# Decay matrix of one attention chunk from a broadcast load instead of matmuls, with a new order table, in a fused mLSTM and two-MoE kernel

## The chip, the cores and the metric

The kernel runs on one core of a Trainium2 chip. A core has TensorE (PE in the profile; PEld is its weight load), VectorE (DVE), ScalarE (ACT), GpSimd (POOL) and SyncE (SP), which here only issues DMAs. The metric is the device time of one execution in microseconds, lower is better.

## The reference, cut to what matters

Three layers follow each other. The first is an attention with gates, written in the reference as a recurrence over 768 tokens for 2 batches and 8 heads of width 40:

```python
for t in range(S):
    m_new = np.maximum(f_gate[:, :, t] + m, i_gate[:, :, t])
    f_stab = np.exp(f_gate[:, :, t] + m - m_new)
    i_stab = np.exp(i_gate[:, :, t] - m_new)
    C = f_stab * C + i_stab * outer(v_t, k_t)
    n = f_stab * n + i_stab * k_t
    y[:, :, t] = sigmoid(o_gate_t) * (C @ q_t) / max(abs(n . q_t), 1)
```

Its 1536 rows of 320 go through `rms` normalisation and a SwiGLU layer (`w_gate`, `w_val` 320x1536, `w_out` 1536x320), and then through a PReLU layer (`w_in` 320x2048, `w_out` 2048x320). The result is 1536x320 in float32.

## The kernel before, in words

The attention is done in 6 chunks of 128 tokens, each for 2 batches: twelve units `u`. For a unit and a head the recurrence becomes a 128x128 matrix of weights `w` (the decay from one token to another, the exponential of a difference of running sums, masked to the past), which multiplies the scores (`sc`, L448) and then the values (`pv`, L502); a state `st` of 40x41 per head carries what lies before the chunk (`pv` from the state at L471, its update at L526). A unit is then normalised on DVE, ACT and POOL, turned on PE (`trxn`, L624) and split into a high and a low half (`xh`, `xl`), since all matmuls of the two MoE layers are made of three products of fp32r halves.

The first MoE layer multiplies per chunk and per pair `p` of 256 columns (`moe1_pair`, L781: 16 products into `g`, 16 into `v`), takes tanh, multiplies, splits the result (`gh` on ACT at L793, `gl` on DVE or POOL at L796) and multiplies by the out weights (`moe1_out`, L787). Chunks 0 and 1 go through it together, since their weights are being made at that time: each block of weights is loaded raw (L662), and ACT and DVE (in part POOL) make its two halves from it (`decode`, L666 to L694). The second MoE layer has 3 x 16 blocks of 512 columns in the same manner (`moe2_chunk`, `moe2_out`).

The decay matrices are made in two ways. With `NB = 2`, chunks 0 and 1 build theirs on PE (`spread` in `prep`, L379 to L391): a product of an identity with a triangular mask (L381), four products that spread a row of `sp` over 128 rows (L384) and one that spreads a column (L389). `sp` holds the running sums of 16 heads as high half in rows 0 to 15 and low half in rows 32 to 47 of 48; ACT writes the high halves (L283), DVE the low ones (L281). One ACT exponential of 128x512 finishes half a unit (L396). From chunk 2 on, the running sums `gA` are written to DRAM (`a_scr`, L318), loaded back to 128 partitions with a broadcast (`load_A`, L407, 512 KB), masked on POOL (L355) and exponentiated per head on ACT with the column as bias (L363); `cols` (L286) then turns one more 16x16 block on PE, and `out_e` copies the column out.

Everything is written as steps of a plan: each call `plan(engine, cost, fn, w, r, take)` gives a step a number, what it writes and reads, and which buffer it takes. Buffers that matter here: 2 of `w`, 2 of `vko` (one load of 484.5 KB per unit), 4 of `r` (two loads of 160 KB per unit), 3 of `stg` (raw weights, mostly 512 KB per load), 1 of `gate`. The order in which the steps are issued is not worked out by the kernel but stands in a table, `ORDER` (from L1024): a number is a step, a trailing `g` puts a step that may run on DVE or POOL on POOL, and `*n` issues `n` filler matmuls of 128 columns (`idle`, L1015, tile `hot`), which are two PE instructions each. Each engine takes its own steps in the order of the table and waits by semaphores for what it reads.

Of the kernel before, what the change touches and what calls it, by code (L numbers as in the profile page):

```python
# [116 lines left out]
def kernel(  # L117
# [15 lines left out]
    nc = tc.nc  # L133
# [58 lines left out]
    def consts():  # L192
# [30 lines left out]
        plan("V", 300, sel, w="sel sp0 sp1", r="ident")  # L223
# [8 lines left out]
    def gates_of(c):  # L232
# [53 lines left out]
        def cols():  # L286
            ps = new(f"gc{c}", "ps", [128, 512])
            if c >= NB:
                nc.tensor.transpose(ps[:, 0:G], T[gt][:, 0, :], ident[:G, :G])
            if c:  # L290
                nc.tensor.transpose(ps[:, G:2 * G], T[gA], ident[:G, :G])
            if 0 < c < NB:
                nc.tensor.matmul(ps[0:DT, 2 * G:3 * G], lhsT=sp_t[c][:, 0, C - 1:C].to_broadcast([48, DT]), rhs=sel_t,
                                 start=True, stop=True)
# [39 lines left out]
    def prep(u):  # L334
# [39 lines left out]
        if c < NB:  # L374
            dec_of(lambda rows, h: T[f"gc{c}"][rows, 2 * G + b * H + h:2 * G + b * H + h + HP, None], f"gc{c}" if c else "")
            for s in range(2):
                ab = f"ab{u}_{s}"

                def spread(ab=ab, s=s):  # L379
                    ps = new(ab, "ps", [128, 4, C])  # L380
                    nc.tensor.matmul(ps, lhsT=idr, rhs=tri_t[:, None, :].to_broadcast([128, 4, C]), start=True, stop=False)  # L381
                    for i in range(4):
                        g = b * H + 4 * s + i
                        nc.tensor.matmul(  # L384
                            ps[:, i], lhsT=sel_t[:, g:g + 1].to_broadcast([48, 128]), rhs=sp_t[c][:, 0],
                            start=False, stop=False
                        )
# [12 lines left out]
                plan("P", tuple(sum(x) for x in zip(mm(1, 512), mm(4, 128, rows=48), mm(1, 512, rows=48))), spread,  # L400
# [3 lines left out]
        else:  # L404
# [31 lines left out]

    def scores(u):
# [15 lines left out]
        plan("P", half(mm(H, 128, rows=40, pairs=True)), prod, w=f"sc{u}_0 sc{u}_1", r=f"{r}/0 {r}/1",  # L453
# [4 lines left out]
    def before(u):  # L458
# [24 lines left out]
        plan("P", half(mm(H, 41, rows=40, pairs=True)), prod, w=f"pv{u}_0/b pv{u}_1/b", r=f"{r}/0 {r}/1 st{b}",  # L483
             take=[("ps", f"pv{u}_{s}", KEEP) for s in range(2)])
        for s in range(2):
# [539 lines left out]
3 7 18 0 19 20 1 2 162 170 26 27 8 9 28 13 5 10 178 11 77 12 14 4 15 16 90 17 *9 35 91 76 99 100 40 21 354 355 163 23  # L1025
22 164 166 171 165 31 172 190 174 24 167 173 168 56 198 25 175 36 169g 176 29 366 37 61 367 34 179 177 38 30 6 32 180
182 33 39 58 55g 57 78 181 *1 53 41 206 44 83g 42 79 59 54 43 80 45 343 81 46 183 60 82 48 184 188 47 *1 74 186 62 191
65 63 84 49 64 86 85 92 109 192 75 87 199 66 185 67 88 200 68 189 187 201 *3 50 93 342 102 89 202 110 214 69 111 133
70 194 207 101 94 203 51 193 204 52 222 119 71 195 95 344 196 205 96 72 208 210 73 348g 215 209 103 97 230 197 146 211
216 105 104 98 217 212 108 112 223 213 106 224 107 135g 132 577 231 114 578 113 117 134 218 238 345 219 115 118 220  # L1030
346 226 566 221 *1 136 232 116 347 123 350 120 349 121 *1 139 160g 137 239 138 122 234 124 225 125 357 159 589 141 126
# [6 lines left out]
456 464 263g 471 465 466 264 458 424 473 472 277 474 298 265g 291 478 475 425 284 279 476 504 285 280 477 286 505 506
310 281 299 292 507 287 490 489 508 288 492 293 509 482 289 300 302 294 311 483 318 301 484 326 295 485 510g 296 491
486 479 480 297 487 481 312 314 493 488 319 567 313 500 495 334 568 494 571 496 303g 327 315 304 502 501 497 308 316  # L1040
522 306 305 498 503 524 320 322 309 523 499 307 428 335 321 525 591 512 430 1117 323 511 514 317 324 513 328 330 515
325 336 338 329 638 516 1125 337 517 518 1133 339g 1118 519 526 520 331 340 521 332 341 527 528 1126 333 1119 529 1127
# [3 lines left out]
685 542 588 703 600 651 686 633 601g 632 627g 636 687 704 705 543 706 555 707 605 556 607 557 606 602 559 560 608 603  # L1046
# [6 lines left out]
791 781 792 812g 813 824 793 782 828 838 794 783 829 795 830 784 840 796 797 839 798 864 803 800 801 802 804 805 841  # L1053
# [100 lines left out]
```

## Time and profile before

| | |
|---|---|
| median of 3 runs | 486.62 us (485.04 to 491.96) |
| the profiled execution | 487.92 us |
| its span, first to last instruction | 486.1 us |
| mean granted TensorE clock | 0.947 |
| PE busy | 479.6 us, 3410 matmuls |
| DVE, ACT, POOL busy | 337.7, 206.8, 58.9 us |

Busy times are the union of an engine's instructions. Matmuls are pipelined, so the own time of one overlaps the next; the distance from one start to the next start is what a matmul costs PE. The granted clock of a stretch is 1.00 (2.4 GHz) or 0.50 (1.2 GHz).

### The profile page before, as it was taken

The page shows a single profiled execution, that of the slowest core. Times are in us where ns is not written, and L with a number is a line of the kernel's source. Part 1 is how long each engine was busy: PE and PEld are TensorE (multiplying, and loading weights), DVE is VectorE, ACT ScalarE, POOL GpSimd, SP SyncE. Part 2 cuts the span into 40 slices and gives each one's busy share as a digit, 9 for nine tenths or more (in the row PEclk, how much of TensorE's full clock was granted, in tenths as well). Part 3 has the DMA queues.
Part 4 walks back from the last instruction along what each step waited for, and adds up shares of the span by engine and source line. Part 5 has one row for each costly group of instructions (what it writes and reads, how often), then busy time and mean ns, then how long its engine had stood idle before and what let it go on. Part 6 is the DMA issues. An engine that isn't in the chain of part 4 may idle for free.

```text
span 486.1 us, 8659 instructions
## 1 busy us (share of the span) xinstructions
PE 479.6 (99%) x3410; PEld 448.2 (92%) x3410; DVE 337.7 (69%) x651; ACT 206.8 (43%) x419; POOL 58.9 (12%) x83
## 2 busy tenths in 40 slices
PE   8999999999999999999999999999999999999997
PEld 7888999999999999999999999889988999898987
DVE  4788788898745745754568799999537475555753
ACT  4485496667471326213525677535103131121211
POOL 1320223231030102102012021202000000000000
PEclk9555699999999999999899999999999999999999
DMA  6864554356520250043006546521001000010001
GB/s 224 300 200 149 200 168 144 105 182 221 142 87 18 70 173 1 19 138 104 34 1 160 178 131 190 166 71 49 1 1 57 15 16 2 0 42 13 1 0 55
DMA packets 18184, 46.56 MB, mean 96 GB/s; under 512 B 2400, under 2 KB 7392, under 8 KB 18144
## 3 DMA queue, kind: packets, MB, share of 16 engines
q1 hardware_dynamic: 18144, 46.01, 29.9%
q8 instruction: 27, 0.44, 0.4%
q14 instruction: 13, 0.11, 0.1%
HBM read 39.02 MB, written 4.36 MB: 89 GB/s over the span
## 4 chain that ended last, share of the span: by engine, by line
PE 93%; DMA 2%; DVE 2%; ACT 1%; issue 0%; POOL 0%; POOLq 0%
PE hm L781 18%; PE accm L787 17%; PE g L781 13%; PE acc L787 13%; PE v L781 12%; PE pv L502 5%; PE sc L448 3%; PE pv L471 2%; PE hot L1018 2%; DMA raw1169w<-in_wi 2%; PE ab L384 2%; PE stp L526 2%; PE trxn L624 1%; PE ab L381 1%; DMA raw1177w<-in_wo 1%; PE ab L389 1%
## 5 line engine op out<-in xcount | busy, mean ns | idle before, releaser
L793 ACT ACTIVATE ghm<-tm 128x512 fp32r<-128x512 f32 x48 | 30.3, 633 | 109.7 <-PE accm L787 90.0
L796 DVE TENSOR_TENSOR glm<-tm,ghm 128x512 fp32r<-128x512 f32 x45 | 30.9, 689 | 41.2 <-ACT ghm L793 35.3
L880 DVE TENSOR_SCALAR tm<-hm,al_sb 128x512 f32<-128x512 f32 x48 | 35.9, 749 | 8.2 <-PE hm L781 6.3
L819 DVE SCALAR_TENSOR_TENSOR t<-t,g 128x512 f32<-128x512 f32 x36 | 24.6, 685 | 21.6 <-ACT t L816 21.2
L816 ACT ACTIVATE t<-g 128x512 f32<-128x512 f32 x36 | 21.4, 595 | 40.1 <-PE g L781 32.8
L793 ACT ACTIVATE gh<-t 128x512 fp32r<-128x512 f32 x36 | 22.4, 630 | 28.0 <-PE acc L787 16.0
L886 DVE SCALAR_TENSOR_TENSOR tm<-hm,tm 128x512 f32<-128x512 f32 x48 | 32.8, 688 | 1.0
L822 DVE SCALAR_TENSOR_TENSOR t<-t,v 128x512 f32<-128x512 f32 x36 | 24.4, 684 | 10.3 <-PE v L781 9.6
L796 DVE TENSOR_TENSOR gl<-t,gh 128x512 fp32r<-128x512 f32 x34 | 24.0, 715 | 9.8 <-ACT gh L793 9.8
L502 PEld LDWEIGHTS pv<-vko,w 128*128 128x128 f32 x192 | 28.4, 229 | 0.8 <-issue 0.4
L502 PE MATMUL pv<-vko,w 128*128 128x41 f32 x192 | 28.8, 313 | 0.0
L363 ACT ACTIVATE w<-w,col 128x128 f32<-128x128 f32 x64 | 20.0, 394 | 0.4 <-DVE col L297 0.3
L452 DVE TENSOR_TENSOR w<-sc,w 128x512 f32<-128x512 f32 x24 | 15.6, 685 | 5.0 <-PE sc L448 3.6
L448 PE MATMUL sc<-r 40*128 40x128 f32 x192 | 17.9, 325 | 0.0
L787 PE MATMUL acc<-o10h,gh 128*128 128x320 f32 x48 | 16.1, 335 | 1.2 <-DVE t L819 1.2
L448 PEld LDWEIGHTS sc<-r 40*128 40x128 f32 x192 | 15.5, 224 | 1.7 <-issue 0.8
L787 PE MATMUL acc<-o12h,gh 128*128 128x320 f32 x48 | 15.9, 331 | 0.0
L787 PE MATMUL acc<-o11h,gh 128*128 128x320 f32 x48 | 15.4, 320 | 0.0
L787 PE MATMUL accm<-o21h,ghm 128*128 128x320 f32 x48 | 15.2, 316 | 0.0
L787 PE MATMUL accm<-o23h,glm 128*128 128x320 f32 x48 | 14.9, 311 | 0.1
L787 PE MATMUL accm<-o20h,glm 128*128 128x320 f32 x48 | 14.9, 311 | 0.0
L787 PE MATMUL accm<-o23h,ghm 128*128 128x320 f32 x48 | 14.9, 310 | 0.0
(498 smaller groups left out, 1647.2 us busy)
## 6 DMA issues: line engine op xcount, KB each, us to landing
vko<-in_vko SPq DMA_DIRECT2D x12, 484.5 KB
w<-a_scr SPq DMA_DIRECT2D x8, 512.0 KB
r<-in_qk SPq DMA_DIRECT2D x24, 160.0 KB
y_scr<-y SPq DMA_DIRECT2D x12, 192.0 KB
x<-y_scr SPq DMA_DIRECT2D x12, 192.0 KB
out<-y SPq DMA_DIRECT2D x12, 160.0 KB
raw206w<-in_wo SPq DMA_DIRECT2D x1, 640.0 KB
raw214w<-in_wo SPq DMA_DIRECT2D x1, 640.0 KB
```

What stands on the lines that cost most here:

```text
L363: nc.scalar.activation(out=T[w][:, h], in_=T[w][:, h], func=AF.Exp, bias=T[f"col{c}"][:, g:g + 1])
L448: nc.tensor.matmul(T[f"sc{u}_{s}"][:, i], lhsT=q[:, 1, i], rhs=q[:, 0, i], start=True, stop=True)
L502: nc.tensor.matmul(ps[:, i, 0:V1], lhsT=T[w][:, h], rhs=v[:, h], start=True, stop=True)
L781: nc.tensor.matmul(ps, lhsT=a, rhs=x, start=(i == 0), stop=(i == len(ops) - 1))
L787: nc.tensor.matmul(a[:, 0:DM], lhsT=g[:, sl], rhs=w[:, j % 4], start=(j == 0 and k == 0), stop=(j == nj - 1 and k == 2))
L793: nc.scalar.activation(out=new(gh, "gh", [128, n], F32R), in_=T[t], func=AF.Copy)
L796: on[e].tensor_tensor(out=new(gl, "gl", [128, n], F32R), in0=T[t], in1=T[gh].bitcast(F32), op=ALU.subtract)
L816: nc.scalar.activation(out=new(t, "t", [128, 512]), in_=T[g], func=AF.Tanh, scale=0.5)
L819: nc.vector.scalar_tensor_tensor(out=T[t], in0=T[t], scalar=1.0, in1=T[g], op0=ALU.add, op1=ALU.mult)
L822: nc.vector.scalar_tensor_tensor(out=T[t], in0=T[t], scalar=0.5, in1=T[v], op0=ALU.mult, op1=ALU.mult)
L880: nc.vector.tensor_scalar(out=new(t, "t", [128, 512]), in0=T[ps], scalar1=0.0, scalar2=al_sb[:, j:j + 1], op0=ALU.min, op1=ALU.mult,)
L886: nc.vector.scalar_tensor_tensor(out=T[t], in0=T[ps], scalar=0.0, in1=T[t], op0=ALU.max, op1=ALU.add)
```

## The change

`NB` becomes 1: chunk 1's decay matrices come by the path of the later chunks (store of `gA`, broadcast load, mask, eight exponentials per unit), and its `spread` steps, its `sp` tile and the `sp` halves go. `sel` and the remaining `sp` tile have 128 rows instead of 48, of which the added ones are zero, so that chunk 0's spreads contract over 128 rows. In `attend` a unit's scores come ahead of its product with the state. The order table is new from end to end.

```diff
-    sel_t = att.tile([48, G], F32R, name="sel")
+    sel_t = att.tile([128, G], F32R, name="sel")
-    NB = 2
-    sp_t = [att.tile([48, 2, C], F32R, name=f"sp{c}") for c in range(NB)]
+    NB = 1
+    sp_t = [att.tile([128, 2, C], F32R, name=f"sp{c}") for c in range(NB)]
...
-                            ps[:, i], lhsT=sel_t[:, g:g + 1].to_broadcast([48, 128]), rhs=sp_t[c][:, 0],
+                            ps[:, i], lhsT=sel_t[:, g:g + 1].to_broadcast([128, 128]), rhs=sp_t[c][:, 0],
                             start=False, stop=False
...
-                        ps, lhsT=sp_t[c][:, 1], rhs=sel_t[:, g:g + 4, None].to_broadcast([48, 4, C]), start=False, stop=True
+                        ps, lhsT=sp_t[c][:, 1], rhs=sel_t[:, g:g + 4, None].to_broadcast([128, 4, C]), start=False, stop=True
...
-                (weighted_v, u), (before, u), (scores, u), (pv, u, 0), (pv, u, 1), (combine, u),
+                (weighted_v, u), (scores, u), (before, u), (pv, u, 0), (pv, u, 1), (combine, u),
...
-3 7 18 0 19 20 1 2 162 170 26 27 8 9 28 13 5 10 178 11 77 12 14 4 15 16 90 17 *9 35 91 76 99 100 40 21 354 355 163 23
+7 0 2 3 1 *4 8 9 10 11 13 14g *7 12 166 174 *1 167 15 168 175 176 77 16 170 17 169 171 177 178 23 21 172 22 24 173 179
...
```

Read by their steps, the two tables give PE this order up to the first product of the first MoE layer (`g0_0`; `u` are units, `I` a filler, a spread is half a unit, a `pv` is half a unit):

```
before: 9 I, sc u0, spread u0, spread u0, spread u1, sc u1, spread u1, pv u0, pv u0, I, state u0,
        pv u1, pv u1, I, state u1, before u2, cols 1, 3 I, turn u0, spread u2, turn u1, spread u2,
        spread u3, spread u3, sc u2, state u2, pv u2, pv u2, I, before u3, I, sc u3, state u3, g0_0
after:  12 I, spread u0, spread u0, sc u0, spread u1, spread u1, sc u1, pv u0, pv u0, pv u1, pv u1,
        state u0, state u1, cols 1, turn u0, sc u2, before u2, turn u1, sc u3, 6 I, g0_0
```

On SP the first loads before are gates, `r` of u0 (two), `vko` of u0, two raw weight blocks; after, gates, two raw weight blocks, `r` of u0 (two). Chunk 1's store and its two broadcast loads stand at places 14, 19 and 28 of SP's queue; the copies that finish the first weight block at 25 and 26, and the gates of chunk 2 ahead of them at 24. On ACT, the decays and four of the eight exponentials of u2 stand ahead of the high half of u1's turned rows. The upper half of chunk 0's `sp` is written on ACT behind the first instruction that reads a raw weight block. Of the 84 low halves `gl` of both MoE layers POOL made 5 before and makes 39 after; of the 39 low halves of weights 3 and 10, of the 39 roundings 6 and 16.

## Rows read from the trace of the kernel before

**Rows 1.** The page: busy time by engine, and PE's granted clock in 40 slices
```profile
PE 479.6 (99%) x3410; PEld 448.2 (92%) x3410; DVE 337.7 (69%) x651; ACT 206.8 (43%) x419; POOL 58.9 (12%) x83
...
PEclk9555699999999999999899999999999999999999
```
**Rows 2.** Waits of PE: engine, line, releaser: us, times, longest
```profile
PE hot L1018 <- POOL ident masks.py:199: 1.7, 1, 1.7
PE acc L787 <- DVE t L819: 1.2, 1, 1.2
```
**Rows 3.** Stretches: length, busy of PE, PEld, DVE, ACT, POOL, PEclk, DMA share, GB/s
```profile
6.70:10.10 3.40, 3.40 (x26) 2.44 (x26) 0.43 (x1) 1.60 (x4) 0.00 (x0) 1.00 0.99 374
10.10:57.90 47.80, 47.80 (x272) 41.03 (x272) 37.72 (x91) 28.50 (x61) 9.92 (x12) 0.50 0.65 209
...
238.80:242.20 3.40, 3.40 (x19) 3.40 (x17) 1.18 (x2) 0.10 (x1) 0.00 (x0) 0.50 0.00 0
```
**Rows 4.** Timeline of PE, 0 to 54: start, own time, operation, count
```profile
1.70 4.21 PE L1018 MATMUL hot<-ident 128*128 128x128 f32 x18 [1.70 <-POOL ident masks.py:199]
5.84 1.86 PE L448 MATMUL sc<-r 40*128 40x128 f32 x16
...
16.72 3.63 PE L502 MATMUL pv<-vko,w 128*128 128x41 f32 x16
20.15 0.78 PE L1018 MATMUL hot<-ident 128*128 128x128 f32 x2
...
27.01 1.93 PE L471 MATMUL pv<-st,r 40*128 40x41 f32 x16
...
29.35 1.65 PE L1018 MATMUL hot<-ident 128*128 128x128 f32 x6
30.79 0.85 PE L624 MATMUL trxn<-ident,xn 128*128 128x128 f32 x3
31.29 0.78 PE L381 MATMUL ab<-tri,idr 128*128 128x512 f32 x1
...
33.57 0.90 PE L624 MATMUL trxn<-ident,xn 128*128 128x128 f32 x3
...
50.44 2.08 PE L448 MATMUL sc<-r 40*128 40x128 f32 x16
...
53.46 0.58 PE L781 MATMUL g<-xh,w10h 128*128 128x256 f32 x1
```
**Rows 5.** Timeline of PE, 70 to 78, at the full clock
```profile
71.70 0.66 PE L526 MATMUL stp<-wv,vko 128*64 128x41 f32 x16
...
72.77 1.09 PE L471 MATMUL pv<-st,r 40*128 40x41 f32 x16
...
76.78 0.98 PE L502 MATMUL pv<-vko,w 128*128 128x41 f32 x8
```
**Rows 6.** Waits of PE's weight loads
```profile
PEld ab L384 <- issue: 3.1, 8, 0.4
```
**Rows 7.** Timelines of SP and ACT, 0 to 14: the first loads and their first reader
```profile
1.53 1.73 SPq L344 DMA_DIRECT2D r<-in_qk  x2
...
3.83 0.42 SPq L662 DMA_DIRECT2D raw162w<-in_wgv  x1
...
8.97 0.67 ACT L666 ACTIVATE raw162w<-raw162w 128x512 f32<-128x512 f32 x1 [0.90 <-DMA raw162w<-in_wgv]
```
**Rows 8.** Waits of POOL, and ACT's exponentials by line (busy, mean ns, idle before)
```profile
POOL w L355 <- DMA w<-a_scr: 4.6, 1, 4.6
...
L363 ACT ACTIVATE w<-w,col 128x128 f32<-128x128 f32 x64 | 20.0, 394 | 0.4 <-DVE col L297 0.3
```
**Rows 9.** Timeline of DVE, 30 to 37: the low half of u1's turned rows
```profile
35.99 0.54 DVE L634 TENSOR_TENSOR xl<-trxn,xh 128x384 fp32r<-128x384 f32 x1
```
**Rows 10.** Groups by line: the low halves of the MoE layers on DVE and POOL
```profile
L796 DVE TENSOR_TENSOR glm<-tm,ghm 128x512 fp32r<-128x512 f32 x45 | 30.9, 689 | 41.2 <-ACT ghm L793 35.3 <-PE accm L787 5.8
...
L796 POOL TENSOR_TENSOR gl<-t,gh 128x512 fp32r<-128x512 f32 x2 | 3.6, 1797 | 10.9 <-ACT gh L793 10.9
```

More of the change, by code (lines that the diff above doesn't have):

```diff
@@ L222, in consts @@
         plan("G", 600, f, w="ident mhalf one gm")
-        plan("V", 300, sel, w="sel sp0 sp1", r="ident")
+        plan("V", 300, sel, w="sel " + " ".join(f"sp{c}/0 sp{c}/1" for c in range(NB)), r="ident")
         plan("G", 300, tri, w="tri", r="ident")
@@ L292, in cols @@
             if 0 < c < NB:
-                nc.tensor.matmul(ps[0:DT, 2 * G:3 * G], lhsT=sp_t[c][:, 0, C - 1:C].to_broadcast([48, DT]), rhs=sel_t,
+                nc.tensor.matmul(ps[0:DT, 2 * G:3 * G], lhsT=sp_t[c][:, 0, C - 1:C].to_broadcast([128, DT]), rhs=sel_t,
                                  start=True, stop=True)
@@ L318, in gates_of @@
             plan("S", dma(8000), lambda: nc.sync.dma_start(out=a_scr[c], in_=T[gA]), w=f"scr{c}", r=gA)
-        if c:
+        if c or c >= NB:
             plan("P", mm(2, 16, rows=16, pairs=True), cols, w=f"gc{c}",
@@ L399, in prep @@
                     at([-100, -99.9, -79.1, -78.9][2 * b + s])
-                plan("P", tuple(sum(x) for x in zip(mm(1, 512), mm(4, 128, rows=48), mm(1, 512, rows=48))), spread,
+                plan("P", tuple(sum(x) for x in zip(mm(1, 512), mm(4, 128), mm(1, 512))), spread,
                      w=ab, r=f"sp{c}/0 sp{c}/1 sel tri", take=[("ps", ab, KEEP)])
@@ L435, in weighted_v @@
         plan("VG", either(328), f, w=f"wv{u}", r=f"vko{u}/vk we{u}", take=[("wv", f"wv{u}")], port=True)
+    scored = {}
     def scores(u):
@@ L452, in weigh @@
             nc.vector.tensor_tensor(out=p, in0=T[f"sc{u}_{s}"], in1=p, op=ALU.mult)
-        plan("P", half(mm(H, 128, rows=40, pairs=True)), prod, w=f"sc{u}_0 sc{u}_1", r=f"{r}/0 {r}/1",
+        scored[u] = plan("P", half(mm(H, 128, rows=40, pairs=True)), prod, w=f"sc{u}_0 sc{u}_1", r=f"{r}/0 {r}/1",
              take=[("ps", f"sc{u}_{s}", KEEP) for s in range(2)])
@@ L482, in scale @@
             )
-        plan("P", half(mm(H, 41, rows=40, pairs=True)), prod, w=f"pv{u}_0/b pv{u}_1/b", r=f"{r}/0 {r}/1 st{b}",
+        i = plan("P", half(mm(H, 41, rows=40, pairs=True)), prod, w=f"pv{u}_0/b pv{u}_1/b", r=f"{r}/0 {r}/1 st{b}",
              take=[("ps", f"pv{u}_{s}", KEEP) for s in range(2)])
+        plan.steps[i][6].add(scored[u])
         for s in range(2):
@@ L1038 @@
[L1038 to L1042, printed above, removed]
[3 rows of a table removed]
@@ new lines @@
+120 118 438 122 127 124 229 125 230 136 143 111 126 138 439 128g 453 355 231 129 130 141 164 142 131 236 370 440 232
+455 362 150 146 148 139 363 364 454 235 357 132 163 144 147 145 149 151 152 356 367 365 154 153 237 155 156 383 386
+441 366 157 158 456 457 368 242 254 360 393 159 238 581 369 385 384 449 450 243 458 239g 451 133 160 391 382 459g 134
+161 240 387 135 162 233 241 388 255 244 256 262 569 371 373 165 246 245 257 247 258 392 374 248 389 442 444 263 270
+249 259 252 250 251 452 471 464 443 473 466 264 445 390 446 375 407g 376 406 410 465 260 408 261 266 394 265 267 379
@@ new lines @@
+1274 1275 1282 1163 1283 1166 1145 1181 1164 1024 1023 1026 1025 1276 1167 1175 1032 1169 1168 1170g 1038 1040 1041
+1284 1033 1035 1039 1037 1034 1066 1036 1042 1171 1172 1176 1177 1178 1183 1067 1043 1277 1148 1323 1044 1068 1189
+1190 1069 1070 1063 1046 1062 1287 1182 1184 1185 1288 1077 1278 1078 1045 1064 1197 1205 1146 979 1179 1180 982 1198
+1279 1186 1187 1188 1191 1199 1048 1065 1280 1200 1201 1202g 1052 1073 1079 1206 1071 1072 1047 1192 1193 1049 1295
+1296 1297 1080 1050 1194g 1074 1203 1298 1204 1081 1195 1207 1299 1099 1075 1100 1084 1076 1290 1357 1213 1225 1101
@@ new lines @@
+1086 1085 1208 1196 1051 1214 1226 1209 1215 1210g 1082 1211 1216 1217 1212g 1102 1083 1088 1087 1233 1241 1227 1095
+1096 1097 1089 1218g 1228 1103 1219 1053 1220g 1054 1234 1090 1091 1235 1237 1229 1230g 1092 1236 1238 1242 1093 1094
+1231 1300 1305 1098 1232 1348 1249 1257 1104 1239 1243 1107 1339 1106 1109 1221 1223 1331 1224 1222 1105 1291 1244
+1245 1246g 1292 1108 1306 1112 1250 1293 1258 1111 1114 1113 1294 1312 1307 1118 1301 1302 1247 1308 1115 1248g 1119
+1309g 1314 1251 1315 1316 1310 1313 1335 1311 1337 1336 1120 1338 1366 1303 1265 1317 1252 1304g 1344 1346 1345 1347
@@ new lines @@
+1240 1259 1261 1340 1341 1318g 1342 1343g 1354 1356 1353 1355 1332 1362 1365 1364 1363 1349 1350 1351 1373 1358 1352
+1367 1359 1360 1361 1253 1254g 1372 1374 1375 1371 1116 1499 1117 1368 1260 1376 1255 1256 1369 1382 1377 1383 1380
+1381 1370g 1392 1389 1390 1391 1384 1500 1401 1393 1487 1378 1266 1379g 1385 1386 1262g 1387 1267 1263 1269 1394 1395
+1388g 1420 1398 1421 1268 1488 1410 1399 1400 1407 1289 1409 1408 1489 1270 1396 1501 1397 1490 1422 1502 1264g 1416
+1418 1417 1324 1427 1402 1327 1319 1419 1426 1425 1428 1320 1403 1404 1405 1321 1423 1325 1322 1406 1333 1271 1411
@@ new lines @@
+1326 1272g 1412 1413 1328 1329 1414 1330 1415g 1429 1436 1434 1435 1437 1334 1444 1447 1430 1446 1443 1445 1431 1432
+1438 1433 1424 1452 1491 1448 1449 1439 1440 1441 1442 1454 1461 1455 1525 1473 1467 1453 1479 1464 1470 1478 1468
+1450 1462 1469 1526 1451 1495 1463 1474 1475 1476 1471 1465 1527 1477 1481 1480 1503 1504 1456 1482 1505 1506 1552
+1457 1458 1459 1460g 1496 1514 1483 1484 1512 1485 1486 1523 1507 1515 1513 1516 1521 1522 1508 1509 1510 1492 1532
+1524 1511 1541 1530 1533 1531 1466 1517 1518 1528 1519 1493 1494 1529 1520g 1534 1553 1535 1536 1539 1540 1543 1542
@@ new lines @@
+1537 1538g 1544 1554 1548 1550 1557 1549 1551 1561 1560 1559 1558 1545 1546 1555 1497 1498 1472 1570 1569 1566 1567
+1568 1547g 1556 1562 1571 1563 1564 1575 1578 1606 1576 1588 1577 1565g 1572 1573 1574 1585 1587 1579 1584 1580 1596
+1586 1607 1608 1581 1582 1583 1593 1615 1594 1602 1605 1603 1614 1595 1597 1611 1609 1610g 1647 1604 1589 1590 1598
+1591 1599 1592g 1612 1650 1613 1641 1622 1620 1623 1600 1601g 1635 1616 1651 1652 1617 1621 1629 1638 1632 1653 1618
+1619g 1654g 1639 1633 1648 1624 1649 1656 1657 1646 1625 1626 1627 1628g 1634 1640 1630 1636 1642 1643 1668 1659 1660
@@ new lines @@
+1661 1658 1655 1644 1645 1667 1664 1665 1677 1666 1673 1662 1663 1674 1675 1676 1686 1682 1685 1683 1695 1684 1669
+1670 1678 1679 1680 1671 1672g 1681g 1692 1691 1694 1722 1700 1693 1701 1702 1710 1711 1704 1637 1631 1696 1687 1688
+1689 1690g 1703 1719 1720 1709 1712 1731 1721 1697 1698 1705 1706 1707 1708 1732 1699 1718 1713 1733 1714 1730 1715
+1740 1728 1739 1729 1727 1716 1717 1734 1735g 1737 1748 1738 1736 1749 1746 1723 1724 1725 1726g 1757 1747 1745 1761
+1741 1755 1754 1759 1756 1758 1760 1750 1742 1751 1743 1744g 1763 1765 1752 1753g 1762 1775 1776 1777 1769 1770 1771
@@ L1093 @@
+1764 1766 1767 1768 1772 1773 1774
 """
```

51 lines of the change are left out of this document (26 added, 25 removed), and 44 rows, old and new, of the table ORDER.

## The prediction

> **What bounds the kernel now.** I read the page first. PE is busy 99% of the span, no other engine more than 69%, and the clock line has five slices near 0.5 right after the first [rows 1]. Then the waits of PE: they are 1.7 us before the first filler and 1.2 us once later [rows 2]. Of the 6.5 us that PE is not busy (486.1 less 479.6) some 3.6 are left, the output after its last matmul. So PE hardly ever waits, and the time is the sum of what its instructions cost at the clock that they get. Third, the stretches: the clock is full from 6.7 to 10.1, half from 10.1 to 57.9, full after that but for 3.4 us at 238.8 [rows 3]. In the half stretch PE is filled without a gap (47.80 of 47.80), while DVE works 37.7 and ACT 28.5 of 47.8 us: PE at the half clock is the bound there, and the others have 10 and 19 us of room. Last, the timeline of PE shows what fills it [rows 4]: attention of chunks 0 and 1 and fillers, until the first product of the MoE layer, g0_0, starts at 53.46. The clock rises 4.4 us later. Whatever moves g0_0 forward or moves work from ahead of it to behind it, where the clock is full, is gained.
>
> **The change, as a walk to g0_0.** I follow the new order of PE at the durations of rows 4, each from one start to the next.
>
> Fillers: 18 records take 4.14 us (1.70 to 5.84), 0.23 each, so 12 fillers (24 records) end at 7.2, or 7.0 if the clock rises at 6.7 again as it did after 5.0 us of this. I take 7.0.
>
> First wait: the first spread needs both halves of sp, and the second one is now behind ACT's first reader of a raw block. Before, that block was issued at 3.83 and read at 8.97, 5.1 us later, with 0.80 MB of r and vko ahead (two loads of 160 KB and one of 484.5); at 374 GB/s these are 2.1 us [rows 3, 7]. Second in SP's queue it is issued at about 1.53 [rows 7]: 4.5, or 5.9 if the next block of 0.5 MB shares the way. ACT's reader takes 0.67 [rows 7], and I allow as much again for the two short operations on 16 rows behind it: 5.8 to 7.2. I take 0.2 us of waiting (0 to 2).
>
> The six groups (four spreads, two scores): they are the same as before, where they took 10.88 us (5.84 to 16.72) with 3.4 us of it at the full clock. I take the same share. The spreads on 128 rows: the weight load of the 48-row product waits 3.1 us over eight spreads for no engine ("issue"), 0.39 each [rows 6]; I take that as the price of going from 128 rows to 48, which goes, so 4 x 0.39 = 1.55 off. Bounds: 0 (the wait has another cause) and 3.1 (it stands again at the last product, L389). The row is nearest to 1.55. The groups then end at 7.0 + 0.2 + 10.88 - 1.55 = 16.5.
>
> The Trainium skill, "TensorE: Matmul & The Clock Gate", section "LDWEIGHTS (loading the stationary operand)", says that a weight load is timed by its columns and that the rows make no difference. By that rule alone nothing is saved here, and the sum below would be 1.55 us smaller; no run so far shows a load of 128 rows in that place.
>
> The rest, all at the half clock: four pv of 3.43 per two (16.72 to 20.15), 6.86. Two scores and two states, 3.02 per pair (50.44 to 53.46), 6.04. Before u2 and cols, 2.34 (27.01 to 29.35). Two turns at 0.50 (30.79 to 31.29), 1.0. Six fillers, 2.8. Together 16.5 + 19.0 = 35.5. So g0_0 starts at 35.5 and not at 53.46: 17.9 us earlier. Four spreads of chunk 1 at 2.28 (31.29 to 33.57), 9.1 us in all, are the largest part of this.
>
> What pays for it behind g0_0: two pv, state u2 and u3 and before u3 now run at the full clock. Their own times there are 0.98, 0.66 and 1.09 [rows 5], so 2 x 0.98 + 2 x 0.66 + 1.09 = 4.4 us at most; less the overlap (3.63 against 3.43 in rows 4) 4.1. Net 13.8.
>
> The clock: the rise came 5.0 us after the first filler and 4.4 us after g0_0 started, both times in unbroken dense work [rows 3, 4]. The six fillers now stand right ahead of g0_0, so the dense work begins at 32.7, the rise is due at about 37.4, 1.9 us behind g0_0's start instead of 4.4. Half of the 2.5 us is gained: 1.2. Net 15.0.
>
> What hides the rest. Chunk 1's new path costs ACT 16 exponentials of 0.39 us against 4 [rows 8], POOL four masks, DVE one copy, DMA 1 MB. The store and load of u2 wait on SP for the buffer of u0 (free when u0's pv end, 16.5 + 3.4 = 19.9). At most 4.6 us for the load [rows 8] gives 24.5. Masks and the four exponentials that ACT has ahead of xh then end at about 28, and the low half of u1's rows is there about 30, 5 us before g0_0 needs it. If that cover is gone, each further us of the load goes into g0_0. DVE had that low half at 35.99 + 0.54 = 36.5 [rows 9], behind 62 steps of its queue; after, 60 stand ahead. It was then waiting for PE (37.7 busy of 47.8), so I expect it earlier, but not by 18 us: this is what is late next. For it, for the first turn (u0's normalisation has only about 6 us of PE work to hide in) and for other joints I allow 1.5 us of new waits. Net 13.5. The later stages have the same products in another order; I cost them at nothing, as PE is the bound with no waits there now.
>
> **The sum.** The profiled execution is 487.92 us, so 487.92 - 13.5 = 474.4. That execution lies 1.3 us above the median of the runs shown (486.62); by the median it would be 473. I predict 474.4, 2.5% below the median.
>
> **The rivals.**
> (a) *The clock stays full longer at the front.* The spreads are denser on 128 rows, and two pairs now stand together. For it: the clock fell at 10.1 after the first scores and two spreads with their 0.39 us holes. Against: pv with its 41 columns follows in any case. One more stretch of 3.4 us at full does the work of 6.8 us: 471; two: 467.6.
> (b) *The feeding takes the bound.* The load of u2, the copies of the first weight block behind chunk 2's gates on SP, or DVE's queue hold g0_0. For it: DVE had its operand at 36.5 with PE much slower. Against: 10 us of room on DVE [rows 3]. If g0_0 waits until 41.5, 6 us of the gain go: 480.4. With nothing left of the gain ahead of g0_0 but the 1.2 of the clock, 486.7.
> (c) *The clock falls again.* After g0_0 the new order mixes pv, states, before and turns with the MoE products; the clock did fall once more late, at 238.8 [rows 3]. A fall costs half of its length: 1.7 us for 3.4, 5 us if it lasts 10: 479.4. Against: state, before and pv stand among the products at 70 to 78 too [rows 5], and the clock line has no slice below 8 or 9 there [rows 1].
> (d) *Slower: POOL's low halves become the bound.* 39 of 84 go to POOL where 5 did. One takes 1.80 us against 0.69 [rows 10]. If PE waits for the difference each of the 34 times, 34 x 1.1 = 37 us come on and the time is 512; with half of that, 493; it eats the whole gain from 13.5 us up, which is 12 of the 34, and makes the change slower from there. The Trainium skill, "SBUF — State Buffer", section "SBUF: two separate sides", says that DVE and GpSimd share a pair of ports by an exclusive lock, the loser standing still for the whole instruction. A mean of 1.80 for the same tile that takes DVE 0.69 agrees with such waits but does not show them. Against (d): the closest such half in the new table has 28 matmuls between its products and its first use, and 22 before, where PE lost nothing.
> (e) *The change doesn't do what it says*: the spreads of chunk 1 were hidden anyway. Rows 2 exclude it: nothing but PE's own work stands there.
>
> **How the numbers follow.** Forecast 0.52, its own range 470 to 479. (a) 0.13, (b) 0.20, (c) 0.08, (d) 0.07. The range: below, (a) with one stretch more and no new waits, 469, a little further for two: 467. Above, (b) without the gain ahead of g0_0: 486. What lies outside is most of (d), the two-stretch end of (a), and the end of (b). About 2% is what a measurement of this kernel can tell from no change, 9.7 us, or 476.9: below it lie 0.44 of the forecast's 0.52, all of (a), 0.03 of (b): 0.60. Slower by over 2% (496) is most of (d) and some mishap of (b): 0.07. The rest, 0.33, is within 2%.
>
> **What would show it.** Right: no 4 spreads after 30 us; g0_0 at 34 to 37; the half clock ends near 37 and not at 57.9; a spread of chunk 0 at half clock costs 1.9 and not 2.3 us, and the "issue" row of L384 is gone; PE still busy 99% with waits under 3 us; ACT's L363 at 80 instructions. Wrong: a wait of PE or its weight load for xl, xh or a weight's copy ahead of g0_0 (b); half-clock slices after 40 us (c); PE waiting for low halves from POOL, with means near 1.8 us (d).

## The result, and the profile after

The changed kernel takes 471.55 us (median of 4 runs, 470.25 to 473.09) beside 487.3 us for the kernel before on the same chip: ratio 0.967 [0.959, 0.974], 15.8 us or 3.3% faster. The forecast of 474.4 was 2.9 us too high. The profiled execution took 471.52 us, its span is 469.7 us (486.1 before). Ratios, here and in the table below, are of fast executions alone (up to 1.5% above the fastest of their kernel) and medians are of all, so the two can differ, as for e9 and e11.

First the page's busy line and clock line, which answer to [rows 1]:

```profile
PE 458.8 (98%) x3390; PEld 433.4 (92%) x3390; DVE 316.7 (67%) x597; ACT 204.6 (44%) x429; POOL 132.2 (28%) x139
...
PEclk9658999999999999999999999999999999999999
```

PE works 20.8 us less and is still busy nearly all the time; the clock line has two slices near 0.5 where it had four. POOL's time has more than doubled, and no other engine has come near the bound. The stretches cut at the clock's edges (columns as in [rows 3]):

```profile
0.00:15.20 15.20, 12.19 (x84) 10.74 (x85) 11.48 (x33) 8.99 (x16) 3.44 (x12) 1.00 0.77 237
15.20:39.10 23.90, 20.64 (x138) 19.23 (x138) 19.80 (x46) 16.89 (x42) 9.24 (x11) 0.50 0.87 275
39.10:469.20 430.10, 425.97 (x3172) 403.46 (x3171) 285.39 (x520) 178.77 (x371) 119.53 (x117) 1.00 0.28 87
```

The 1.00 of the first line holds from 5.0 us on: up to there the fillers follow each other at 0.21 us, then at 0.11. 47.8 us at half clock have become 23.9. But in them PE is no longer filled: 20.64 of 23.90, where it was 47.80 of 47.80. The late fall at 238.8 us is not there. What PE stands for now shows in its waits (as [rows 2], the three largest):

```profile
PE trxn L627 <- ACT xn L610: 2.9, 2, 1.6
PE hot L1021 <- POOL ident masks.py:199: 1.4, 1, 1.4
PE sc L450 <- DMA r<-in_qk: 1.0, 2, 0.7
```

And the timeline of PE up to the first MoE product, g0_0, to be laid beside [rows 4]:

```profile
5.78 0.48 PE L381 MATMUL ab<-tri,idr 128*128 128x512 f32 x1
...
14.77 3.18 PE L505 MATMUL pv<-vko,w 128*128 128x41 f32 x16 [0.41 <-DMA vko<-in_vko]
...
25.38 0.90 PE L627 MATMUL trxn<-ident,xn 128*128 128x128 f32 x3 [1.23 <-ACT xn L610]
...
31.54 0.90 PE L627 MATMUL trxn<-ident,xn 128*128 128x128 f32 x3 [1.62 <-ACT xn L610]
...
34.78 2.93 PE L1021 MATMUL hot<-ident 128*128 128x128 f32 x12
37.36 0.56 PE L784 MATMUL g<-xh,w10h 128*128 128x256 f32 x1
```

g0_0 starts at 37.36 instead of 53.46, 16.1 us earlier. PE's last matmul, before (first line) and after (second):

```profile
482.55 0.31 PE L787 MATMUL accm<-o23h,glm 128*128 128x320 f32 x1
```

```profile
466.01 0.31 PE L790 MATMUL accm<-o23h,glm 128*128 128x320 f32 x1
```

From the start of g0_0 to the end of this one the time is 429.0 us and was 429.4. So nearly the whole gain lies ahead of g0_0; the work that was moved behind it has its cost, but other things there became cheaper by as much (told below).

### The profile page after: what moved, and what is told of

Same layout as the page of the kernel before. It is cut to its first block, busy times and chain, and to the rows that moved or that the text cites. A ratio compares the mean times of both kernels' runs of the same rounds, so it can differ in the third digit from the quotient of the medians.

```text
span 469.7 us, 8674 instructions
## 1 busy us (share of the span) xinstructions
PE 458.8 (98%) x3390; PEld 433.4 (92%) x3390; DVE 316.7 (67%) x597; ACT 204.6 (44%) x429; POOL 132.2 (28%) x139
## 4 chain that ended last, share of the span: by engine, by line
PE 82%; DMA 7%; DVE 6%; ACT 2%; issue 1%; SPq 0%; POOL 0%; DVEq 0%; POOLq 0%; ACTq 0%
PE hm L784 19%; PE accm L790 18%; PE g L784 12%; PE v L784 12%; PE acc L790 12%; PE pv L505 3%; DMA raw218w<-in_wo 2%; PE sc L450 2%; DMA raw202w<-in_wgv 2%; PE pv L473 1%; DMA w15h<-rlw 1%; DMA w<-a_scr 1%; DMA raw174w<-in_wgv 1%; PE trxn L627 1%; PE stp L529 1%
## 5 line engine op out<-in xcount | busy, mean ns | idle before, releaser
L799 POOL TENSOR_TENSOR glm<-tm,ghm 128x512 fp32r<-128x512 f32 x26 | 34.7, 1339 | 102.2 <-ACT ghm L796 101.3
L883 DVE TENSOR_SCALAR tm<-hm,al_sb 128x512 f32<-128x512 f32 x48 | 35.7, 748 | 40.3 <-POOL glm L799 21.8
L799 POOL TENSOR_TENSOR gl<-t,gh 128x512 fp32r<-128x512 f32 x13 | 17.9, 1379 | 53.8 <-ACT gh L796 52.8
L799 DVE TENSOR_TENSOR glm<-tm,ghm 128x512 fp32r<-128x512 f32 x22 | 15.4, 704 | 19.3 <-ACT ghm L796 19.3
L363 ACT ACTIVATE w<-w,col 128x128 f32<-128x128 f32 x80 | 26.1, 392 | 2.8 <-DVE col L297 2.2
L505 PEld LDWEIGHTS pv<-vko,w 128*128 128x128 f32 x192 | 26.0, 211 | 1.1 <-issue 0.6
L505 PE MATMUL pv<-vko,w 128*128 128x41 f32 x192 | 26.2, 295 | 0.8 <-DMA vko<-in_vko 0.4
L799 DVE TENSOR_TENSOR gl<-t,gh 128x512 fp32r<-128x512 f32 x23 | 17.4, 757 | 7.2 <-ACT gh L796 7.2
L587 POOL TENSOR_TENSOR ss<-ss,mhalf 128x1 f32<-128x1 f32 x12 | 7.8, 652 | 50.8 <-ACT xn L581 44.5
L355 POOL TENSOR_SCALAR_AFFINE_SELECT w<-w 128x512 f32<-128x512 f32 x20 | 13.6, 696 | 17.1 <-ACT dec L370 17.1
L450 PEld LDWEIGHTS sc<-r 40*128 40x128 f32 x192 | 14.5, 210 | 3.4 <-issue 1.3
L790 PE MATMUL acc<-o11h,gh 128*128 128x320 f32 x48 | 15.8, 330 | 0.0
```

The source lines that it names most:

```text
L363: nc.scalar.activation(out=T[w][:, h], in_=T[w][:, h], func=AF.Exp, bias=T[f"col{c}"][:, g:g + 1])
L450: nc.tensor.matmul(T[f"sc{u}_{s}"][:, i], lhsT=q[:, 1, i], rhs=q[:, 0, i], start=True, stop=True)
L505: nc.tensor.matmul(ps[:, i, 0:V1], lhsT=T[w][:, h], rhs=v[:, h], start=True, stop=True)
L790: nc.tensor.matmul(a[:, 0:DM], lhsT=g[:, sl], rhs=w[:, j % 4], start=(j == 0 and k == 0), stop=(j == nj - 1 and k == 2))
L799: on[e].tensor_tensor(out=new(gl, "gl", [128, n], F32R), in0=T[t], in1=T[gh].bitcast(F32), op=ALU.subtract)
L883: nc.vector.tensor_scalar(out=new(t, "t", [128, 512]), in0=T[ps], scalar1=0.0, scalar2=al_sb[:, j:j + 1], op0=ALU.min, op1=ALU.mult,)
```

## The experiments

My theory after this reading had three parts: the path takes chunk 1's four spreads off PE, the rows keep the clock full longer, and the table puts chunk 1's products where the clock is full. The rivals: one of the three does it all; or the path is hidden anyway. All medians below are of timed runs, beside the kernel before on the same chip.

| run | edit | us | before | ratio to before |
|---|---|---|---|---|
| e8 | the change, again | 471.55 | 487.41 | 0.967 [0.963, 0.971] |
| e1 | the change on 48 rows | 472.38 | 486.83 | 0.970 [0.967, 0.974] |
| e10 | the change without the path | 476.64 | 487.08 | 0.978 [0.975, 0.981] |
| e2 | before on 128 rows | 484.38 | 486.83 | 0.993 [0.990, 0.995] |
| e3 | before with the path | 490.63 | 486.83 | 1.007 [1.004, 1.010] |
| e9 | e3, two products first | 490.67 | 487.08 | 1.004 [1.001, 1.008] |
| e11 | e9 on 128 rows | 491.94 | 487.08 | 1.004 [1.000, 1.009] |
| e12 | e11, the load's wait behind | 490.33 | 487.53 | 1.007 [1.003, 1.010] |
| e4 | the change, low halves on DVE | 473.24 | 486.83 | 0.972 [0.969, 0.976] |
| e5 | the change, turns reordered | 471.42 | 487.41 | 0.968 [0.964, 0.972] |
| e6 | the change, six fillers out | 470.63 | 487.41 | 0.968 [0.964, 0.972] |
| e7 | e5 and e6 together | 470.14 | 487.41 | 0.966 [0.962, 0.970] |

### The rows: 48 in the new table, 128 in the old

```diff
-    sel_t = att.tile([128, G], F32R, name="sel")
+    sel_t = att.tile([48, G], F32R, name="sel")
```

and so in `sp_t` and the two spread products (e1); the opposite edit in the kernel before (e2).

> The changed kernel with the selector, the split scans and chunk 0's spreads back on 48 rows; the new table stays, and nothing else is changed. Theory (128 rows count): the 0.39 us holes ahead of the second spread of a group come back, the granted clock falls again a few us after the feeding matrices end (in the kernel before: full from 6.7 to 10.1 us, in the changed one from 5.0 to 15.2), later spreads take 1.7 to 2.2 us instead of 1.0 to 1.3, and the first MoE product starts at 40 to 42 us instead of 37.4: the whole is 3 to 6 us slower than the changed kernel, 475 to 478 us. Rival (the number of rows is of no account, the gain is the removed work of chunk 1 alone): no holes or holes that other waits would have filled, the first product within 0.5 us of 37.4, the whole within 1 us of 471.5.

> The kernel before, with its old table and both chunks' decay on TensorE, and only the selector and the split scans on 128 rows instead of 48. Theory (128 rows count): the eight spreads of both chunks lose their holes of 0.39 us and the granted clock stays full beyond 10.1 us; the first MoE product, at 53.5 us in the kernel before, starts 3 to 8 us earlier, and the whole is 3 to 8 us faster than the kernel before, 479 to 484 us. Rival (rows are of no account): within 1 us of the kernel before.

In the old table the rows are worth 2.4 us, in the new one 0.8 us or nothing (the intervals of e1 and e8 overlap). Both show the mechanism. The weight loads' wait of [rows 6] is back in e1 (first line) and absent on 128 rows. The stretch at full clock in the front is 3.4 us in e1 (second line), 10.2 in the profile after and 6.8 in e8; in e2 there are two of 6.9 and 6.8 (third and fourth), the first of which comes later (13.9) than the one of before (6.7):

```profile
PEld ab L384 <- issue: 1.1, 3, 0.4
```

```profile
7.20:10.60 3.40, 3.40 (x29) 2.78 (x28) 3.19 (x6) 2.53 (x6) 0.00 (x0) 1.00 0.83 220
```

```profile
13.90:20.80 6.90, 6.48 (x70) 5.84 (x69) 6.80 (x18) 3.57 (x7) 3.23 (x3) 1.00 0.81 245
...
31.00:37.80 6.80, 3.99 (x32) 3.23 (x31) 5.52 (x11) 5.25 (x10) 1.18 (x1) 1.00 0.85 264
```

What a hole costs PE can be read from start to start at the half clock: a spread takes 1.71 us in e2 (10.66 to 12.37) and took 2.28 before (31.29 to 33.57 in [rows 4]):

```profile
10.66 0.64 PE L381 MATMUL ab<-tri,idr 128*128 128x512 f32 x1
...
12.37 0.63 PE L381 MATMUL ab<-tri,idr 128*128 128x512 f32 x1
```

So e1's theory has the holes and the clock right and the size wrong: g0_0 starts at 38.4 and not at 40 to 42. That lies between its two starts on 128 rows, 37.36 after and 38.84 in e8. PE, slower by the clock, then hardly stands for the turns. Their wait is 0.5 us in e1:

```profile
PE trxn L627 <- ACT xn L610: 0.5, 1, 0.5
```

Ahead of g0_0 PE stands 3.1 us in sum in e1, 6.3 after and 5.8 in e8. What PE loses at half clock is time in which it would have stood, mostly for ACT. In e2 g0_0 starts at 50.67, 2.8 us earlier than before; that and the 2.4 us of the whole are a little less than the 3 to 8 of its theory. New waits of PE appear (2.4 us for ACT's `o10h`, 1.9 for DVE's `xl`) and take part of the gain.

### The path without the order, and the order without the path

e3 keeps the old table and puts the new steps at the places of those that they replace: the store (84) and loads (91, 103) as soon as their data and buffers are free, masks and exponentials where spreads and exponentials stood (the numbers shift with `NB = 1`):

```diff
-... 43 80 45 343 81 46 183 60 82 48 184 188 47 ...
+... 43 80 45 347 81 84 91 46 187 60 103 48 188 192 47 ...
```

e10 is the changed kernel with `NB = 2`, unit 2's spreads ahead of unit 1's turn and unit 3's behind g0_0.

> The kernel before with chunk 1's decay taken from the broadcast load, 48 rows as before, and the old table with the new steps put in at the places of the steps that they replace: the path alone, without the search's order. Theory (the removed TensorE work pays): some 16 us of half-clock spreads and their scores' accumulations leave the stretch before the first MoE product, chunk 1's products wait for the store and the two loads in part, and 4 to 9 us of it reach the end: 478 to 483 us. Rival (the path only pays with the new order; in the old one chunk 1's exponentials come too late and TensorE stands for them): 484 to 490 us, with waits of TensorE for the masked decay of chunk 1 of over 5 us in sum. A third reading (the order is worth nothing, all is in the path and the rows): 472 to 476 us.

> The changed kernel, 128 rows and new table, with chunk 1's decay back on TensorE: unit 2's two spreads stand ahead of unit 1's turn, unit 3's behind the first MoE product; store, loads, masks and GpSimd's part are gone. Theory (the path is worth what TensorE would spend: 4 us of spreads at half clock, part of them in the turn's wait, and 2.2 at full clock or 4.4 at half): first product at 39 to 41 us, the whole 474 to 478 us, so the order alone would give some 10 of the 16 us. Rival (the order is worth nothing without the path): 482 us or more. Third (the removed TensorE work was hidden): within 1 us of 471.5.

The path alone makes the kernel 3.8 us slower, although PE is busy 10 us less. PE's waits in e3:

```profile
PE stp L526 <- DVE wv L432: 6.9, 1, 6.9
PE trxn L624 <- ACT xn L607: 3.2, 1, 3.2
PE pv L502 <- ACT lwraw226w L673: 2.1, 1, 2.1
```

These are 12.2 us, and g0_0 starts at 57.35, 3.9 us later than before. The second of the waits has a plain cause in ACT's timeline; the others were not followed. The decays (L370) read the broadcast load; they stand at their old places, wait for it, and unit 1's scaled rows (L607) stand behind them in ACT's queue:

```profile
30.74 0.44 ACT L370 ACTIVATE dec<-w 64x4 f32<-64x4 f32 x2 [1.56 <-DMA w<-a_scr]
33.42 0.44 ACT L370 ACTIVATE dec<-w 64x4 f32<-64x4 f32 x2 [2.25 <-DMA w<-a_scr]
...
34.09 0.80 ACT L607 ACTIVATE xn<-vko,ss 128x320 f32<-128x320 f32 x2
```

The rival of e3 holds; the time passes its 484 to 490 us by 0.6. e10 then falls into its theory's range (474 to 478): the new order is worth some 8 us with chunk 1's decay still on PE (e2 484.4 against e10 476.6), and the path 5 us more on top (e10 against e8; the intervals do not meet). With the 2.4 us of the rows these are 15 of the 15.8 us. The places of the steps put in are by hand in both runs, so other places could give other numbers. In e10 unit 2's spreads fill the wait for unit 1's turn, another wait stands behind it (1.17 us for `xl`), and g0_0 starts at 40.65, 3.3 us later than after:

```profile
33.78 0.85 PE L627 MATMUL trxn<-ident,xn 128*128 128x128 f32 x3
35.80 2.34 PE L450 MATMUL sc<-r 40*128 40x128 f32 x16 [1.17 <-DVE xl L637]
...
40.65 0.56 PE L784 MATMUL g<-xh,w10h 128*128 128x256 f32 x1
```

### Can the path's waits be mended by hand?

If the order only has to give PE work that is ready, two steps moved should do. e9 puts g0_0 and v0_0 (435, 436) ahead of unit 2's state (136); e11 adds the 128 rows; e12 puts the decays (92, 104) behind the turns' chain. From e3's table to e12's:

```diff
-... 50 92 346 104 87 ... 69 ... 70 ... 51 ... 52 ... 71 ... 72 ... 73 ... 116 ... 136 ... 435 ... 436 ...
+... 50 69 70 51 71 72 52 73 92 346 104 87 ... 116 ... 435 436 136 ...
```

> The path alone with one thing more: of the old table two steps, the first two MoE products (of which the first started at 57.4 us with the path alone), stand ahead of unit 2's state product on TensorE, where it stood 6.9 us for chunk 1's value rows. Theory (the path frees TensorE, and the order only has to put work there that is ready): the first product starts at 40 to 42 us, the clock rises by 45 us instead of 61, and the whole is 474 to 480 us, 10 us or more below the path alone. Rival (the search's gain is spread over the whole table, these two steps are a small part of it): 484 to 488 us.

> The run with the path and the two products moved ahead, and the selector and split scans on 128 rows as well: all of the change but the new table. Theory (rows keep the clock full beyond 10 us, worth 2.4 us in the old table): 1 to 3 us below the same on 48 rows. Rival (as in the new table, the feeding engines take it): within 1 us of it.

> The run with the path, 128 rows and the two products moved ahead, and the two decay steps of chunk 1 (ScalarE, which stood 4.4 and 1.4 us for the broadcast load) put behind unit 0's and unit 1's scaled rows and roundings, which waited behind them; the roundings' low halves on VectorE move with them. Theory: that wait in ScalarE's queue is why TensorE stood 5.2 us for unit 1's rows and began the first product at 40.3 us: now the waits for the rows are under 2.5 us in sum and the first product starts at 33 to 36 us; but the steps behind it stand as they stood in the old table, on all engines, so the lead is lost again by the 60th product (72.0 us in the run without this, 69.6 in the kernel before), and the whole stays at 484 to 492 us. Rival (the wait for the load was all that held the old order): the whole falls to 476 to 482 us.

e9's time refutes its theory. How it came is read from e11, which has the same order (its profiled execution took 487.55 us, e9's 495.74): g0_0 starts at 40.35, 13 us earlier than before, with PE still 5.2 us late for unit 1's rows. e11 is no faster than e9, as its rival had it. The clock rises at 44.7 and falls again at 51.5, after PE has turned back to chunk 1's state, values and scores (from 46.5 on):

```profile
44.70:51.50 6.80, 5.51 (x66) 5.17 (x64) 5.27 (x15) 4.60 (x11) 0.74 (x1) 1.00 0.35 107
51.50:65.10 13.60, 11.52 (x73) 10.73 (x72) 12.56 (x34) 7.62 (x18) 3.18 (x5) 0.50 0.69 234
```

e12 comes out as its theory said: the wait for the rows is gone, the whole stays in 484 to 492 us. Another wait stands in its place, the copy that completes the first weight block:

```profile
PE g L781 <- DMA w10h<-rlw: 5.0, 1, 5.0
PE pv L502 <- ACT lwraw226w L673: 2.5, 1, 2.5
...
PE trxn L624 <- ACT xn L607: 0.4, 1, 0.4
```

g0_0 starts at 33.74 there, earlier than in any other run (six of its 16 matmuls run, then the wait), and e12 is still 3 us slower than before. How the lead is lost can be counted: matmuls of L781 (L784 in the changed kernel) that started in the first 55 and 75 us, in the stretches of before, after and e12:

```profile
0.00:55.00 55.00, 1.54 (x7) 0.59 0.63 205
0.00:75.00 75.00, 10.52 (x66) 0.68 0.66 209
```

```profile
0.00:55.00 55.00, 9.40 (x64) 0.78 0.74 235
0.00:75.00 75.00, 21.75 (x160) 0.84 0.73 228
```

```profile
0.00:55.00 55.00, 6.06 (x32) 0.71 0.70 212
0.00:75.00 75.00, 11.27 (x58) 0.70 0.67 208
```

At 55 us e12 leads by 25 matmuls, at 75 it is 8 behind. The two products that were moved were all that was ready: the next stands behind chunk 1's work in the old order, and that runs at half clock (in e12 from 50.5 to 67.5). After 55 us the changed kernel goes on with products; it has 64 by then. So the start of g0_0 was a good measure only because the new table keeps up behind it.

### GpSimd's low halves

```diff
-... 243 458 239g 451 133 160 391 382 459g 134 ...
+... 243 458 239g 451 133 160 391 382 459 134 ...
```

and so at all 39 places (239 is no low half of the MoE layers).

> The changed kernel with the 39 low halves of the MoE's rounding that the table gives to GpSimd done by VectorE instead, everything else in the same order. Theory (these halves on GpSimd bound nothing in the new table): the time stays within 1 us of the changed kernel's 471.5, VectorE's busy time grows by 27 to 30 us (39 of about 0.72 us) and GpSimd's falls by 53 us. Rival (the low halves on GpSimd, 1.34 us each, are what the products wait for late): 2 to 6 us faster. Third reading (VectorE is the nearer bound): 1 to 5 us slower, with waits of the products for VectorE's low halves.

473.24 us: not faster, so the rival is out: GpSimd's halves bound nothing. The intervals of e4 and e8 overlap, so the 1.7 us by which e4's median lies above are not told from nothing, and the third reading is not excluded. The page of e4:

```profile
PE 460.7 (97%) x3390; PEld 434.4 (92%) x3390; DVE 334.3 (70%) x636; ACT 205.1 (43%) x429; POOL 82.4 (17%) x100
```

POOL falls by 50 us, but DVE grows by 17.6 and not by 27 to 30. The halves themselves add 26.2 us to DVE (84 take 59.1 us in sum, 45 took 32.9 after), and DVE's other 552 instructions take 5.9 us less (308.1 for 314.0), which is told below; the rest is that neighbours overlap, and the busy time is their union.

### What still holds the front of the new table

ACT's timeline after the change names the late one of the two turns' operands. A raw weight block of the output product is taken up (L669) when its load lands, and unit 1's rows stand behind it:

```profile
29.82 0.76 ACT L669 ACTIVATE raw218w<-raw218w 128x640 f32<-128x640 f32 x1 [1.55 <-DMA raw218w<-in_wo]
...
30.92 0.80 ACT L610 ACTIVATE xn<-vko,ss 128x320 f32<-128x320 f32 x2
```

```diff
-... 85 346 86 206 66 211 50 67 51 212 214 207 75 54 52 113 116 208 219 92 69 68 190 70 209 ... 71 ... 72 ... 73 ...
+... 85 346 86 206 66 54 75 211 113 50 116 67 212 214 207 208 51 69 68 190 70 92 71 72 219 209 52 73 ...
```

(e5; 219 is that block, 50 and 71 the turns, 113 and 116 unit 2's scores and state products.) e6 takes the `*6` ahead of 435 out of the table, e7 does both.

> The changed kernel, unchanged, as the measure for the three runs beside it: 470 to 473 us, the first MoE product at 37 to 38.5 us, two waits for the scaled rows of 2 to 4 us in sum.

> The changed kernel with a dozen steps moved ahead of the first MoE product: unit 2's scores and state products stand before unit 0's turn on TensorE, ScalarE scales unit 1's rows before it takes up the weight of L669 whose load lands at 29.8 us, and the roundings follow their turns. Nothing is added or left out. Theory (the feeding engines' order holds the first product, TensorE stands 2.9 us for the turns): the two waits vanish, the first product starts 2 to 3 us earlier, at 34.5 to 35.5 us, and the whole is 1.5 to 3 us faster than the changed kernel beside it. Rival (chunk 1's masked decay and its load hold what follows, so the waits only move behind the first product): first product earlier, but TensorE then stands for the weights of unit 2, the whole within 0.7 us.

> The changed kernel without the six idle matrices (2.86 us of TensorE at half clock) that stand ahead of the first MoE product; these matrices feed no result. The second rounded half of the rows that this product waits for ended at 34.6 us, the product started at 37.4. Theory (they only delay it): first product at 34.8 to 35.2 us, the whole 1 to 2.5 us faster. Rival (they bring the clock's rise, which came 4.3 us after their first and 1.8 us after the first product): the rise comes some 4 us after the first product instead of 1.8 and at about the same moment, 39 us; the products before it run at half clock, and the whole is between 0.5 us faster and 1 us slower. Third: without them the clock stays low past 45 us, 2 to 5 us slower.

> Both edits: the steps moved and the six idle matrices left out (they feed no result). Theory (feeding order and idle matrices both hold the first product): it starts at 32 to 33 us, the whole is 3 to 5 us faster than the changed kernel. Rival (behind the first product the chain of chunk 1's decay, its masks at 31 to 37 us and its value rows, is late): TensorE stands 2 us or more for unit 2's weights, the whole 0 to 2 us faster.

None is told apart from the change, and g0_0 doesn't start where the theories had it: at 38.23 in e5 (34.5 to 35.5), at 35.64 in e7 (32 to 33). In e5 the turns' wait falls from 3.1 to 1.0 us (e8 beside it), and waits for the load of `r` (2.1 us instead of 1.2), for `gm` and for `xl` (1.2 each) take its place. In e6 g0_0 starts at 35.55, 1.8 us earlier than after, while the clock rises at 39.0, the moment at which it rose with the fillers (39.1):

```profile
33.57 2.04 PE L450 MATMUL sc<-r 40*128 40x128 f32 x14 [0.63 <-DMA r<-in_qk]
35.55 0.58 PE L784 MATMUL g<-xh,w10h 128*128 128x256 f32 x1
```

So the first products run longer at half clock, as the rival of e6 has it; the 0.9 us measured against e8 lie between the theory's and the rival's and are inside the scatter. e7 is 470.1 us, the lowest median of all; it cannot be called better.

## Why the prediction was right

*The walk to g0_0* was right in sum. It gave 35.5, and with the 1.5 us allowed for new waits 37.0; measured 37.36 (38.84 in e8, the same program). That it agrees so well is in part luck, since two sizes were off against each other. The fillers ended at 5.8 and not at 7.0, as the first began 0.3 us earlier and the clock rose at 5.0 and not at 6.7; the six groups took 9.0 us (5.78 to 14.77) where 0.2 + 10.88 - 1.55 = 9.5 were reckoned, 1.6 us of it waits (0.95 for `r`, 0.4 for `vko`, 0.3 for `sp`). So pv began 1.7 us early. Then the rest took 22.6 us instead of 19.0, and of these 3.6 the stops ahead of the two turns are 2.9 and that ahead of the second pv 0.4. "u0's normalisation has only about 6 us of PE work to hide in" had named the place, and the allowance of 1.5 was half of what it took.

*Rival (a)* came in its condition and not in its price: the full clock lasted from 5.0 to 15.2, two stretches of 3.4 us more than reckoned, for which it gave 467.6. By e1, with one stretch, this is worth 0.8 us at most, for the reason given there.

*The rows.* The 0.39 us for a hole was about right: the holes are there on 48 rows in both tables and on no profile with 128, and a spread without one is 0.4 to 0.6 us shorter at the half clock (1.87 and 1.71 in e2 for 2.28). What the rows change is not how long a load of weights takes: at the full clock 182 to 187 ns with 48 rows (before) and 187 to 192 with 128 (after). That agrees with the Trainium skill, "TensorE: Matmul & The Clock Gate", section "LDWEIGHTS (loading the stationary operand)", by which rows make no difference to a load. The hole is idle time ahead of the load. But as a term of the sum it was not the change's: e1 keeps all but 0.8 us of the gain without it, since ACT's rows would have been waited for instead (on this reading of e1's waits).

*What pays for it behind g0_0* was right at 4.1 us: from start to start the two pv of u2 take 1.70 us there (40.13 to 41.83), state u2 0.59, before u3 1.02 and state u3 0.58, in sum 3.9:

```profile
40.13 1.87 PE L505 MATMUL pv<-vko,w 128*128 128x41 f32 x16
41.83 0.36 PE L784 MATMUL v<-xh,w10h 128*128 128x256 f32 x1
...
43.92 0.66 PE L529 MATMUL stp<-wv,vko 128*64 128x41 f32 x16
44.51 1.09 PE L473 MATMUL pv<-st,r 40*128 40x41 f32 x16
45.53 0.39 PE L784 MATMUL g<-xh,w11h 128*128 128x256 f32 x1
```

*"The later stages have the same products in another order; I cost them at nothing"* is the term that was mis-sized, and it makes up the 2.9 us of the error (3.3, less the 0.4 by which g0_0 came later than 37.0). With the 1.2 of the clock, what follows g0_0 was to become 2.9 us longer; it became 0.4 us shorter. So the other work there took 4.3 us less. Of these, 1.3 are the earlier rise of the clock (1.7 us behind g0_0 instead of 4.4), as forecast. Another 1.7 are the late fall at 238.8 of [rows 3], which did not come and was not counted as a gain. Shorter waits of PE are 0.3. The last us was not traced.

*That removed work of PE is worth its own time* was the step that failed as an account, though the total hides it. The prediction walked the new order as a whole, called PE's four removed spreads, 9.1 us, "the largest part", and left feeding to a rival. By e2, e3 and e10 the order alone gives 8 us, the path gives 5 with it and takes 4 without it, at the places tried. Rival (b), feeding as the bound, is what e3 shows; it was given 0.20 and prices of 480 to 487, and e3 paid more than these, 490.6. Rival (c) came in e11 and e12, whose clock falls again for 13.6 and 17.0 us, and not in the change.

*Rivals (d) and (e).* POOL's halves took 1.34 and 1.38 us each in place of the 1.80 of [rows 10], and e4 shows that nothing hangs on them:

```profile
L799 POOL TENSOR_TENSOR glm<-tm,ghm 128x512 fp32r<-128x512 f32 x26 | 34.7, 1339 | 102.2 <-ACT ghm L796 101.3
...
L799 POOL TENSOR_TENSOR gl<-t,gh 128x512 fp32r<-128x512 f32 x13 | 17.9, 1379 | 53.8 <-ACT gh L796 52.8
```

No wait of PE for one of them is in its waits; DVE does wait 21.8 us for them, which costs nothing. The spreads were not hidden: e10, with them, is 5 us slower.

Of the marks that the prediction set, no spread after 30 us, the vanished "issue" row, L363 at 80 instructions and no low clock after 40 us are there. g0_0 at 37.36 is just outside 34 to 37, and the half clock ends at 39.1 and not near 37. "Waits under 3 us" is not there: the ten largest of PE's are 7.5 us, and it is busy 98%. Spreads of 1.9 us at the half clock can be seen in e2 and e10 (1.7 to 1.9), not after, where all of them ran at the full one. One reading of the rows was wrong without effect: the clock line of [rows 1] has four slices near 0.5, not five.

What stays open: why the 48-row load leaves a hole, why the rows change how long the full clock lasts, and which of the new table's many moved steps behind g0_0 the 8 us need. e12 shows only that three sorts of them, moved by hand, are not enough.

## What to carry to other kernels

An edit that frees the bounding engine is worth what the order of all engines lets it be worth: with the old order the freed time turned into 12 us of waits, with a new one it gave 5 us. When a first product starts earlier, count also the products done 20 and 40 us later; a lead that the next steps can't follow is lost. A step that waits for a load delays, in an in-order queue, the steps behind it that another engine needs sooner; moving it took PE's wait from 7.3 us (e11) to 0.4 (e12), but gained no time while other waits stood behind it.

## What the runs showed that I had not expected

The full clock in the front depends on the rows of the spreads: in all four profiles on 48 rows (before, e1, e3, e9) the front has 3.4 us of it, on 128 rows 6.8 or 10.2 in one piece, and the same program had 10.2 us in one execution and 6.8 in another (after, e8).

Low halves on GpSimd slow some of DVE's other instructions. DVE's 552 instructions other than the halves took 314.0 us in sum after and 312.5 in e8, and 308.1 in e4, where GpSimd has no halves. Single ones show it plainly: an operation on 8 columns that begins during one of GpSimd's halves (after, first and second line) took 1.28 us and ended 0.04 us behind it; in e4 (third line) the same one took 0.16. In e8 it took 1.27.

```profile
68.27 1.28 DVE L555 TENSOR_SCALAR rd<-hn 128x8 f32<-128x8 f32 x1
```

```profile
67.92 1.59 POOL L799 TENSOR_TENSOR gl<-t,gh 128x512 fp32r<-128x512 f32 x1 [3.32 <-ACT gh L796]
```

```profile
71.53 0.16 DVE L555 TENSOR_SCALAR rd<-hn 128x8 f32<-128x8 f32 x1
```

This agrees with the exclusive lock that the Trainium skill names ("SBUF — State Buffer", section "SBUF: two separate sides"); it costs DVE time that it has to spare here.
